# A hand-scheduled attention and FFN kernel: another written order of all steps, and one of four PSUM copies given to ScalarE

## The chip, the cores and the metric

The kernel runs on one core of one Trainium2 chip. The metric is device microseconds of one execution; lower is better. A core has a matrix engine (TensorE, PE in the profile; its weight loads are shown apart as PEld), VectorE (DVE), ScalarE (ACT), GpSimd (POOL) and SyncE (SP, which here only issues DMAs). Each takes its own instructions in the order in which they were written, and waits on semaphores for the others. All of them share 16 DMA engines.

## What is computed

Nystrom attention on q, k, v of shape (8 batches, 8 heads, 576 tokens, 64), followed by a gated FFN without an activation:

```python
q_lm, k_lm = means of 18 rows in a group      # 32 landmarks
A = sm(q, k_lm); Bm = sm(q_lm, k_lm); C = sm(q_lm, k)
Z = start from Bm; six times: Z = 2 * Z - Z @ Bm @ Z
attn = A @ Z @ C @ v
x = attn as (4608, 512)
out = ((x @ w1) * (x @ w2) @ w3) @ w_out      # d_ff 1024
```

## The kernel before, in words

The kernel folds w3 and w_out into one matrix w34, since nothing stands between them, and folds (Z C v) of each batch with w1 and w2 into a matrix G, so that the FFN's two up projections are A times G. All of it is cut into small generators, one for each step; each `yield` ends a part of a step. A string, `ORDER` (lines 32 to 86), lists words such as `U3.1`; the loop at line 661 takes them one by one, starts the word's generator where it stands for the first time and runs it to its next `yield` each time. Nothing else orders the work: on each engine, instructions stand in the order in which the words emit them (`tc.manual_schedule`, line 117), and waits are put in by the framework where buffers or data ask for them.

The words, with the number of their batch or block after the dot:

- `H`, `LO`, `L`, `P`: loads of w3 and w_out in blocks of 128 rows (lines 569, 578, 587, 623; SP's queue, three of them ACT's). w3 blocks go round three places, so block 5 (`L.5`) can only be fetched when block 3 has been transposed (`T0.3`, `T1.3`). `GT` (line 621) is a tiny copy on POOL that reads a loaded block, so that what follows on POOL's queue is not issued before that block is there; the next load into that place also waits for this copy.
- `S`: the split of w_out into two f16 parts (lines 510, 512). `T`: transpose of half a w3 block on PE and its split (lines 525, 529, 531). `F`: product of a block, eight parts of three matmuls, then one copy (lines 539, 542). `K`: one matmul on zeros (line 596); seven more stand ahead of everything.
- `LK`, `LQ`: load of half of k or q of a batch, cast to f16 on the way (line 126, POOL's queue). `TK`, `TQ`: transpose on DVE (line 163). `SK`, `SQ`: landmark sums, on DVE for batch 0 and on POOL for the others (lines 192 to 203). `E`: exchange of landmarks between partitions (lines 210 and 214 for batches 0 and 1; four ACT copies at 221 for the others).
- `B`, `N`, `R`, `I0` to `I5`: Bm, its norms, and the inverse by six iterations (lines 239 to 255, 288, 304, 387 to 406), for the batches of a chain together: (0), (1, 2), (3, 4), (5, 6, 7). A step of `I` is matmuls, then a DVE sum (394), then an ACT copy (400), and the next step's matmuls need both.
- `C`: landmark scores against k (lines 267, 278, 282). `LV`, `FV`: loads of v in four pieces (lines 145, 150, SP's queue). `V`: C v, three parts of PE work (line 344). `Z`: times the inverse (413, 419, 421).
- `A`: scores against the landmarks (323, 330). `M`: their softmax, on DVE (362 to 373).
- `G0` to `G3`: the four blocks of G (line 436: 32 matmuls of a 64x32 shape into a two-bank PSUM tile `big`, then one copy of 128x1024 to f16). `project(st, i)` takes n = i // 2 (the half of d_ff) and w = i % 2 (w1 or w2). G0 and G2 (w = 0) are copied by ACT (line 441), G1 and G3 by DVE (line 443).
- `U0` to `U7`: one eighth of d_ff: four matmuls for w1 into `big` (451), an ACT copy `a_sb` (456), four matmuls for w2, a DVE product (459). U0 to U3 need G0 and G1, U4 to U7 need G2 and G3.
- `W`: 128 rows of the output: eight matmuls (494) in two parts, an ACT copy (500), two DMAs (505). W.35 is cut in two halves (475 to 489).

PSUM holds three `big` tiles and two `one` tiles, so a new `big` waits until an earlier one has been copied out. `qkn` and `vt` have two buffers each.

## Time and profile before

| | |
|---|---|
| runs | 258.41, 258.57 and 256.64 us, median 258.41 us |
| profiled execution | 258.62 us |
| its span, first to last instruction | 256.8 us |
| matmuls on PE | 4448 |
| instructions in all | 10255 |
| read from HBM / written | 38.80 MB / 9.44 MB |
| mean granted clock of PE | 0.993 |

The span is cut into stages by time; "busy" is the union of an engine's instructions in a stage. A row of waits names the instruction that stood idle, what released it, and the idle time. The word "issue" stands where an engine waited for nothing that the profile shows. A row of the timeline gives start, length, engine, line, operation, tiles, and in brackets the idle time before it. The chain of waits follows the end of the execution back, step by step, to what released it.

### The profile page before, as it was taken

What the parts mean: (1) busy time and instruction counts of PE and PEld (TensorE: products, weight loads), DVE (VectorE), ACT (ScalarE), POOL (GpSimd) and SP (SyncE); (2) the same over time, 40 slices, a digit from 0 to 9 for tenths busy, and PEclk for the clock granted to TensorE, in tenths of its full rate; (3) what the DMA queues carried; (4) which work ended last, traced back from release to release, by engine and by line L of the source; (5) the groups of instructions that cost most, each with busy time, mean ns of one, the idle gap of its engine ahead of it and who ended that gap; (6) DMA issues with size and microseconds to landing.
All of it is one profiled execution on the core that took longest, in us unless ns stands there. A gap on an engine that the chain in (4) does not pass through costs nothing.

```text
span 256.8 us, 10255 instructions
## 1 busy us (share of the span) xinstructions
PE 244.3 (95%) x4448; PEld 144.7 (56%) x4448; DVE 182.5 (71%) x348; ACT 140.8 (55%) x317; POOL 117.9 (46%) x199
## 2 busy tenths in 40 slices
PE   7799999997689999999999999999999999999993
PEld 2345545553356646656664766655665646646651
DVE  2689887757658998887998768666958668735410
ACT  4534542457135687766575798457436762654531
POOL 8035799999729996599989930000000000000000
PEclk9799999999999999999999999999999999999999
DMA  6999998999967829799697034444642205313165
GB/s 228 272 309 255 264 246 195 218 222 210 154 94 185 131 35 173 169 204 175 127 189 205 5 89 87 103 123 95 163 96 59 71 3 128 82 42 83 41 146 142
DMA packets 23356, 37.36 MB, mean 145 GB/s; under 512 B 2832, under 2 KB 11536, under 8 KB 23312
## 3 DMA queue, kind: packets, MB, share of 16 engines
q1 hardware_dynamic: 12768, 23.99, 36.8%
q0 software_dynamic: 9792, 11.54, 28.2%
q10 hardware_dynamic: 752, 1.18, 1.5%
q8 instruction: 35, 0.57, 0.9%
q14 instruction: 9, 0.07, 0.1%
HBM read 38.80 MB, written 9.44 MB: 188 GB/s over the span
## 4 chain that ended last, share of the span: by engine, by line
PE 78%; DMA 11%; DVE 4%; issue 2%; SPq 2%; POOL 1%; ACT 0%; POOLq 0%; DVEq 0%
PE big L451 26%; PE one L494 22%; PE one L539 7%; PE big L436 6%; DMA vt<-in_v_dram 5%; PE big L344 5%; DMA qkn<-in_k_dram 5%; PE big L387 4%; PE big L494 1%; PE one L413 1%; PE big L267 1%; PE big L323 1%; SPq L150 1%; DMA out_dram<-o_sb 1%; PE one L304 1%
## 5 line engine op out<-in xcount | busy, mean ns | idle before, releaser
L451 PE MATMUL big<-eat,gt 128*128 128x288 f16 x512 | 75.6, 287 | 3.1 <-issue 3.1
L451 PEld LDWEIGHTS <-gt 128*128 128x128 f16 x512 | 47.7, 98 | 27.4 <-issue 6.9
L456 ACT CAST a_sb<-big 128x576 f16<-128x576 f32 x64 | 40.4, 642 | 41.0 <-PE big L451 30.8
L192 POOL TENSOR_TENSOR tr<-qkT 128x256 f32<-128x256 f16 x56 | 36.1, 673 | 14.6 <-DVE qkT L163 14.1
L494 PE MATMUL one<-w,aby 128*128 128x512 f16 x144 | 36.9, 380 | 0.0
L459 DVE TENSOR_TENSOR abx<-a_sb,big 128x576 f16<-128x576 f16 x32 | 23.6, 748 | 16.7 <-PE big L451 11.8
L539 PE MATMUL one<-abx,w3t 128*128 128x512 f16 x120 | 30.9, 386 | 0.0
L494 PE MATMUL one<-w,abx 128*128 128x512 f16 x120 | 30.2, 379 | 0.0
L459 DVE TENSOR_TENSOR aby<-a_sb,big 128x576 f16<-128x576 f16 x32 | 23.3, 742 | 8.4 <-PE big L451 7.1
L443 DVE TENSOR_SCALAR gt<-big 128x1024 f16<-128x1024 f32 x16 | 19.4, 1218 | 8.0 <-PE big L436 7.9
L163 DVE STREAM_TRANSPOSE qkT<-qkn 128x576 uint32<-128x576 uint32 x32 | 23.9, 756 | 0.9 <-DMA qkn<-in_k_dram 0.9
L500 ACT ACTIVATE o_sb<-one 128x512 f32<-128x512 f32 x33 | 19.6, 600 | 8.3 <-PE one L494 8.3
L494 PEld LDWEIGHTS <-aby 128*128 128x128 f16 x144 | 13.1, 98 | 14.0 <-issue 4.0
L441 ACT ACTIVATE gt<-big 128x1024 f16<-128x1024 f32 x16 | 16.1, 1024 | 8.0 <-PE big L436 7.9
L198 POOL TENSOR_TENSOR tr<-tr 128x256 f32<-128x256 f32 x28 | 20.3, 747 | 0.1
L494 PEld LDWEIGHTS <-abx 128*128 128x128 f16 x136 | 13.0, 98 | 11.8 <-issue 0.4
L436 PE MATMUL big<-wup,zt 64*32 64x512 f16 x512 | 18.8, 379 | 0.0
L539 PEld LDWEIGHTS <-w3t 128*128 128x128 f16 x120 | 11.2, 99 | 12.0 <-issue 0.9
L344 PE MATMUL big<-vt,ent 64*32 64x64 f32 x1152 | 16.2, 223 | 1.6 <-DMA vt<-in_v_dram 1.6
L344 PEld LDWEIGHTS big<-vt,ent 64*32 64x32 f32 x1152 | 13.5, 105 | 6.9 <-issue 5.5
L539 PE MATMUL one<-abx 128*128 128x512 f16 x60 | 16.5, 396 | 0.0
L278 ACT ACTIVATE en<-big 128x288 f32<-128x288 f32 x32 | 12.8, 415 | 4.7 <-PE big L267 4.7
(193 smaller groups left out, 344.8 us busy)
## 6 DMA issues: line engine op xcount, KB each, us to landing
out_dram<-o_sb SPq DMA_DIRECT2D x68, 128.0 KB, 2.4
qkn<-in_k_dram POOLq DMA_DIRECT2D x16, 288.0 KB, 6.5
qkn<-in_q_dram POOLq DMA_DIRECT2D x16, 288.0 KB, 6.6
vt<-in_v_dram SPq DMA_DIRECT2D x16, 288.0 KB, 6.2
vt<-in_v_dram SPq DMA_DIRECT2D x32, 144.0 KB, 4.9
w3f<-in_moe_w_dram SPq DMA_DIRECT2D x5, 512.0 KB, 8.6
wup<-in_moe_w_dram POOLq DMA_DIRECT2D x4, 512.0 KB, 10.8
aby<-in_moe_w_out_dram SPq DMA_DIRECT2D x6, 256.0 KB, 8.2
```

The lines of the kernel that those rows point to most:

```text
L163: nc.vector.transpose(out=st["qkT"][:, t, prs].rearrange("p c r q e -> p (c r q e)").bitcast(U32), in_=st["qkn"][:, t, prs, :].rearrange(" ...
L192: add(out=tr[:, c], in0=x[:, c, 0:4, :], in1=x[:, c, 4:8, :], op=ALU.add)
L198: add(out=tr[:, c, 0:2, :], in0=tr[:, c, 0:2, :], in1=tr[:, c, 2:4, :], op=ALU.add)
L344: nc.tensor.matmul(psV[32 * o:32 * o + 32, qd, 0:64], ent[sl, pr, r, :], vt[sl, pr, 64 * r:64 * r + 64], start=(r == 0), stop=(r == RT - 1 ...
L436: nc.tensor.matmul(psG[o:o + 32, qd, :], zt[rs, i, h, :], wup[rs, h, w, fs], start=(i == 0), stop=(i == 1), tile_position=(64 * qd, o))
L443: nc.vector.tensor_scalar(out=g[:, :, w, fs], in0=psG, scalar1=X64 / ZS, scalar2=None, op0=ALU.mult)
L451: nc.tensor.matmul(p[:, c, 0:HS], st["g"][:, qd, w, 128 * j:128 * j + 128], st["ahat", qd][:, c, :], start=(qd == 0), stop=(qd == 1))
L456: nc.scalar.copy(out=a_sb, in_=p[:, :, 0:HS])
L459: nc.vector.tensor_tensor(out=st["ab"][:, j, st["t0"]:st["t0"] + S].rearrange("p (c s) -> p c s", c=2), in0=a_sb, in1=p[:, :, 0:HS], op=AL ...
L494: nc.tensor.matmul(pso[:, :], ab[:, j, t0:t0 + 128], w34[:, j, :], start=(j == 0), stop=(j == 7))
L500: nc.scalar.activation(out=o_sb, in_=pso, func=AXF.Copy, scale=1.0 / (X64 * X64))
L539: nc.tensor.matmul(psW, w3ts[j, c // 4][:, a, c % 4, :], wsp[:, b, c, :], start=(c == 0 and a + b == 0), stop=(c == 7 and a == 1))
```

## The change

All 53 lines of `ORDER` are written anew. Both orders hold the same words, each the same number of times. One condition in `project` changes: the block with n = 1 and w = 1 (G3) is copied by ACT too. So ACT has three of the four copies of each batch, DVE one.

```diff
 ORDER = """
-H.0 LO.0 KC T0.0 H.3 LO.3 KC LK1.0 H.1 K AT LO.1 T0.0 T0.1 KC S.0 T0.1 H.2 S.0 LO.2 T0.1 T1.0 LQ0.0
-KC F.1 T0.0 S.1 F.0 S.1 LK0.0 S.2 LQ1.0 S.3 T1.0 S.2 T0.0 LO.5 F.1 H.4 K T1.0 T0.0 LO.4 F.0 T0.0
...
-LK0.2 T1.3 F.2 T0.3 E.0 GT.3 TK1.1 F.2 T1.3 P.4 B.0 F.2 FV.0 C.0 B.0 L.5 LQ0.2 B.0 T0.4 F.2 N.0 F.3
...
-T0.7 G0.0 T1.7 B.1 F.6 LK1.4 T1.7 F.6 M1.0 B.1 V.1 G3.0 M1.0 B.1 G0.0 U0.0 F.6 N.1 F.6 G3.0 V.1 G1.0
-U0.0 N.1 U1.0 U1.0 M0.1 F.7 G1.0 R.1 U0.0 TQ1.3 U3.0 R.1 LQ1.4 F.7 U0.0 U3.0 V.1 G2.0 R.1 TQ0.3
...
+H.0 K H.1 H.3 K LO.1 H.4 K LO.4 LO.0 T0.1 LO.2 KC LO.3 T0.0 KC H.2 AT S.0 S.0 K T0.1 GT.0 K T0.0 S.1
+T0.1 KC LO.5 T0.0 T1.1 T0.0 F.0 T1.1 F.1 S.1 L.2 LO.6 F.1 T0.0 T1.0 S.2 LO.7 LK1.0 S.4 T0.0 S.2 T1.1
+LK0.0 GT.2 LQ0.0 S.3 S.3 S.4 T1.0 F.0 F.1 LQ1.0 P.4 T1.0 S.5 LQ1.1 S.6 T0.2 F.0 S.5 F.0 S.7 T0.2 S.6
...
+F.2 LK0.2 F.2 T0.3 E.0 F.2 F.3 F.3 KC TQ0.1 LK1.2 L.5 E.0 LK0.1 B.0 B.0 T1.3 C.0 TQ1.1 F.3 B.0 F.3
+N.0 T0.4 T0.4 N.0 SQ0.1 F.3 C.0 A.0 C.0 R.0 C.0 TK1.1 R.0 F.3 T1.4 R.0 F.3 A.0 I0.0 F.3 A.0 I0.0
+T0.5 T1.4 T0.5 F.4 GT.4 LQ1.2 T1.4 LQ0.2 TK0.1 F.4 I0.0 C.0 M0.0 F.4 FV.0 F.4 T0.5 M0.0 I1.0 I1.0
...
+T1.7 G2.0 G1.0 F.6 G3.0 T0.7 G0.0 E.2 TK1.3 M0.1 C.1 E.2 SK0.3 G1.0 F.7 F.7 G0.0 C.1 B.1 U5.0 M1.1
+LV3.3 G3.0 F.7 V.1 U5.0 U5.0 LK1.4 U1.0 F.7 U5.0 TQ0.3 U1.0 V.1 TK0.4 B.1 U0.0 U1.0 U0.0 F.7 LQ1.4
...
+F.7 I0.1 SK1.3 LQ0.4 U3.0 I0.1 M0.1 TK1.4 F.7 I0.1 I1.1 U4.0 I1.1 I1.1 U4.0 U2.0 U4.0 I2.1 I2.1 I2.1
+U7.0 SQ0.3 I3.1 U2.0 I3.1 U7.0 SQ1.3 I3.1 U6.0 LK0.5 U7.0 U6.0 F.7 LV1.2 U7.0 SK0.4 SK1.4 U6.0 U6.0
...
+SQ0.7 G0.4 U5.3 U2.3 W.9 M0.4 G0.4 C.5 U2.3 SQ1.7 G1.4 W.9 SK0.7 C.5 W.10 M1.4 C.5 U2.3 SK1.7 M0.4
+E.7 U3.3 LV0.5 G1.4 M1.4 U2.3 C.5 E.7 LV0.6 U4.3 B.5 W.9 U3.3 U4.3 U3.3 C.5 B.5 U0.4 U6.3 U3.3 W.10
+U6.3 U6.3 B.5 N.5 U6.3 V.5 V.5 N.5 G3.4 W.13 M0.5 M1.5 LV1.6 U0.4 G3.4 W.11 W.10 U0.4 W.13 M1.5 U3.4
...
 """
...
         yield
-        if w == 0:
+        if w == 0 or n:
             nc.scalar.activation(out=g[:, :, w, fs], in_=psG, func=AXF.Copy, scale=X64 / ZS)
         else:
             nc.vector.tensor_scalar(out=g[:, :, w, fs], in0=psG, scalar1=X64 / ZS,
```

In the new order, PE does the same 4448 matmuls, K among them; the DMAs are the same in number and size, issued in another order on SP's, ACT's and POOL's queues.

## The prediction

> **What bounds the kernel now.** I read the page first, then the busy time by stage, then the waits, and last the timeline at the two stages that the table picked out.

> ```profile
> span 256.8 us, 10255 instructions
> ...
> PE 244.3 (95%) x4448; PEld 144.7 (56%) x4448; DVE 182.5 (71%) x348; ACT 140.8 (55%) x317; POOL 117.9 (46%) x199
> ...
> q8 instruction: 35, 0.57, 0.9%
> ```
> ```profile
> 0.00:12.20 12.20, 8.92 (x30) 4.05 (x31) 5.51 (x17) 5.88 (x11) 5.33 (x19) 0.86 0.87 249
> 60.00:72.00 12.00, 7.24 (x197) 4.06 (x182) 7.14 (x13) 4.10 (x14) 8.78 (x14) 1.00 1.06 177
> 64.30:68.30 4.00, 3.96 (x129) 2.44 (x130) 2.57 (x6) 1.13 (x2) 3.77 (x7) 1.00 1.01 147
> 71.40:250.00 178.60, 178.58 (x3579) 109.70 (x3579) 130.37 (x234) 107.45 (x235) 66.29 (x103) 1.00 0.53 110
> ```
> ```profile
> PE big L451 <- issue: 3.1, 1, 3.1
> ...
> PE big L525 <- DMA w3f<-in_moe_w_dram: 2.0, 1, 2.0
> ...
> PE big L344 <- DMA vt<-in_v_dram: 1.6, 1, 1.6
> ```

> In the stages, the first two numbers are the stage and PE's busy time in it. From 71.4 to 250 us PE is busy 178.58 of 178.60 us: there TensorE is the bound and nothing can be gained by order, only lost. What an order can win lies ahead of that: the start, where PE is busy 8.92 of 12.2 us at a granted clock of 0.86, and the stage from 60 to 72 us, where it is busy 7.24 of 12.

> ```profile
> 62.38 0.32 PE L344 MATMUL big<-vt,ent 64*32 64x64 f32 x10
> 64.32 0.58 PE L344 MATMUL big<-vt,ent 64*32 64x64 f32 x36 [1.62 <-DMA vt<-in_v_dram]
> 67.86 0.42 PE L451 MATMUL big<-eat,gt 128*128 128x288 f16 x2
> 71.42 0.41 PE L451 MATMUL big<-eat,gt 128*128 128x288 f16 x2 [3.14 <-issue]
> ```

> That stage holds two stops of PE: 1.62 us in V.1, until the last piece of v of batch 1 landed, and 3.14 us in the middle of a U, between matmuls that wait for nothing. I take the second for missing instructions: the instruction queue brings 0.57 MB in 35 packets, which is one packet for 127 of the 4448 matmuls, and 129 matmuls ran in the 4.0 us just ahead of the stop, with the DMA engines full (share 1.01). That is an inference; no row names it.

> **The change, part by part.** PE's own work is the same 4448 matmuls. Prices by row, from the chain of waits:

> ```profile
> 65.98 0.65 PE one L539 x3
> ...
> 79.36 0.98 PE big L451 x8
> ...
> 89.81 0.86 PE one L494 x4
> ...
> 94.48 0.56 PE big L436 x16
> ...
> 105.89 0.99 PE big L436 x32
> ...
> 152.83 0.81 PE one L239 x48
> ```

> *Turns between shapes.* Sixteen L436 take 0.56 us, sixteen more 0.43: an entry into the small shapes costs 0.13 us. Counted through the two lists of PE's instructions, turns between full and small shapes go from 120 to 124 (+0.5 us), turns among small shapes from 37 to 32 (up to -0.6 us). I take 0, between -0.6 and +0.5.

> *The wait for v of batch 1.* Ahead of V.1 the new order puts twelve more F matmuls (4 x 0.65 = 2.6 us), 16 each of G2, G1 and G3 (3 x 0.56 = 1.7 us; a whole block is 32, so up to 3 x 0.99 = 3.0) and a U half (0.49): 4.8 to 6.1 us. SP issues the last pieces behind L.7, which waits for GT.5 at the end of about the same POOL work as before. So the wait of 1.62 us is covered three times: -1.6, and 0 if those loads come 6 us later.

> *The instruction stop.* The same count of packets, 128 matmuls each, in the new order: the packet that takes in V.1 holds 38 small ones of G and B, 48 and 18 of V, 12 F and U, and 12 of F, and lasts 6.4 us by these prices against 4.8 in the old order; the shortest between 40 and 100 us lasts 5.2. The old stop began after 4.0 us and ended after 7.1 (71.42 - 64.3). With fewer loads behind it by then I take -3.1. If a packet again takes 7.1 us, 0.7 us of it stays (7.1 - 6.4); if it is no matter of packets, all 3.1 stay.

> *The start.*

> ```profile
> 8.34 1.49 PE L539 MATMUL one<-abx 128*128 128x512 f16 x3
> 9.62 1.49 PE L539 MATMUL one<-abx,w3t 128*128 128x512 f16 x3
> ...
> 13.24 0.81 PE L539 MATMUL one<-abx 128*128 128x512 f16 x3
> ```
> ```profile
> 27.48 0.38 PE L210 MATMUL big<-lm,pick 128*128 128x256 f16 x2 [0.27 <-DVE lm L203]
> ```

> The old start loses 2.0 us for a piece of w3, and six F matmuls at half speed, 2 x (1.49 - 0.81) = 1.4 us. In the new order all pieces of w3 and w_out stand ahead of q and k on the queues (LK1.0 waits for GT.0, LQ0.0 for GT.2), so the weights come sooner and q, k of batch 0 later; 2.4 us more PE work (nine F matmuls and a T) stands ahead of E.0, where PE last waited for VectorE at 27.48. But T0.2 now comes before half of F.0, and waits for a 512 KB block. Best: -3.4; worst: +2.0, the same wait once more. I take -0.6, near the middle.

> [...]

> *SP's queue.* v of batch 0 now stands behind L.5, which waits for T1.3.

> ```profile
> 27.28 9.54 SPq L573 DMA_DIRECT2D w3f<-in_moe_w_dram  x2
> ...
> 43.15 1.10 PE big L344 x72
> ```
> ```profile
> DMA to landing us min/median/max: 4.1/9.3/13.6
> ```

> T1.3 comes about 1.7 us of PE work ahead of E.0, so near 27.5 us, as L.5 did before. Six issues of some 0.65 us end at 31.5, and land 4.1 to 13.6 us later: 35.6 to 45.1, at the median 40.8. V.0 has 1.5 us less PE work ahead of it than before (an F part and two I steps), so stands at 43.15 - 1.5 - 0.6 = 41.0. I take 0, up to +4.1.

> *G3 on ScalarE, and thin places.*

> ```profile
> L443 DVE TENSOR_SCALAR gt<-big 128x1024 f16<-128x1024 f32 x16 | 19.4, 1218 | 8.0 <-PE big L436 7.9
> ...
> L500 ACT ACTIVATE o_sb<-one 128x512 f32<-128x512 f32 x33 | 19.6, 600 | 8.3 <-PE one L494 8.3
> ...
> L441 ACT ACTIVATE gt<-big 128x1024 f16<-128x1024 f32 x16 | 16.1, 1024 | 8.0 <-PE big L436 7.9
> ```
> ```profile
> 149.13 0.41 ACT L278 ACTIVATE en<-big 128x288 f32<-128x288 f32 x1 [0.15 <-PE big L267]
> ...
> 150.04 0.63 ACT L456 CAST a_sb<-big 128x576 f16<-128x576 f32 x1
> ...
> 151.49 1.67 ACT L221 COPY lm<-lm 32x256 f16<-32x256 f16 x4
> ...
> 157.16 0.19 ACT L247 ACTIVATE one<-one 128x32 f32<-128x32 f32 x1
> ...
> 159.30 1.18 ACT L456 CAST a_sb<-big 128x576 f16<-128x576 f32 x2
> ```
> ```profile
> 159.19 0.19 DVE L251 RECIPROCAL rbs<-rbs 128x6 f32<-128x6 f32 x1 [0.59 <-ACT one L247]
> 159.42 0.36 DVE L253 TENSOR_TENSOR bm<-one,rbs 128x192 f32<-128x192 f32 x1
> ```
> ```profile
> 84.02 0.45 PE L387 MATMUL big<-sz__1434,tz__1421 32*32 32x64 f32 x32
> ...
> 85.64 0.45 PE L387 MATMUL big<-sz__1462,tz__1457 32*32 32x64 f32 x32
> ...
> 87.11 0.35 PE L387 MATMUL big<-sz__1511,tz__1497 32*32 32x32 f32 x32
> ```

> VectorE loses 8 x 1.22 = 9.7 us, ScalarE gains 8 x 1.02 = 8.2 us: 149 of 257, still far from full. Neither is at the bound on the whole, so this alone is worth 0; it costs where PE soon needs what lies behind such a copy. Queued behind it are the copies a_sb, and PE for their PSUM. The tightest place I found is N.5, which needs B.5's exponentials. From C.5's matmuls on, ScalarE has U2.3 (0.63), W.9 (0.60), C.5 (2 x 0.91), E.7 (1.67), U3.3 (0.63) and B.5 (157.16 to 159.30, 2.1): 7.5 us, then 0.6 on VectorE: 8.1. PE has G1.4 (0.99), W.10 (1.72), five U halves and one more pair (7 x 0.49 = 3.4) and B.5 (0.81): 6.9. PE waits 1.2 us there. Second, a step of the inverse takes 1.47 to 1.62 us from matmul to matmul; I1.1 to I2.1 to I3.1 in the new order have 0.45 + 0.65 and 0.45 + 0.49 us of PE work on the way from I0.1 and I2.1: 0.4 + 0.5 short. Places with less than 1.3 us of PE work between the release of a `big` and its next use go from 16 to 24; I add 0.2 for them. Short stops: +2.3 in all; at least 0 (ScalarE and VectorE may have run ahead), at most 8.2, each new copy in full.

> **Sum.** -1.6 - 3.1 - 0.6 + 2.3 = -3.0 us. The profiled execution took 258.62 us, 1.8 more than its span, and lies 0.2 over the median of 258.41. So 255.6 us, span 253.8. Within 1% means 255.8 to 261.0, about what a measurement of this kernel can tell from no change.

> **Rivals.**
> 1. The 3.14 us stop stays, there or at another dense place: -1.6 - 0.6 + 2.3 = +0.1, 258.7 us. For it: the packets are inferred. Against it: the thinner packets. [...]
> 2. Slower: ScalarE's in-order queue. G3's copies stand ahead of a_sb copies that PE needs at once. If each of the eight is paid in full, +8.2 in place of +2.3: -5.3 + 8.2 = +2.9, 261.5 us. It decides from 5.3 us of short stops on, 0.66 us a copy. For it: the 1.2 us at N.5. Against it: the old order had stretches where ScalarE was as full, with PE busy 178.58 of 178.60 us.
> 3. v of batch 0 lands last, behind L.5: +4.1 at most, 259.7 us; at 3 us, 258.6. Two fifths of the range of landings lie past 41.0.

> **How the numbers follow.** The forecast has 0.42, rival 1 0.17, rival 3 0.11, rival 2 0.30. Faster by over 1%: 0.42; within 1%: 0.28; slower: 0.30. Low end: all gains (-1.6 - 3.1 - 1.4) and no short stops, 252.5. High end: rival 2's 261.5 and 0.5 for turns, 262.0.

> **What would show it.** Right: no idle PE over 0.5 us between 55 and 75 us, V.1 without a wait for v, PE idle for about 1 us ahead of L288 of the last chain (near 155 us) and twice 0.4 ahead of L387 between 75 and 85. Wrong: an "issue" row of 2 us or more on PE; PE waits for L441 that add up to over 5 us; V.0 waiting for v near 41 us; a PE idle by more than 3 us between 5 and 30 us.

## The result, and the profile after

The changed kernel takes 256.31 us (median of 20 executions, 253.58 to 259.71) where the kernel before takes 257.99 (20 executions, 256.37 to 259.79): a ratio of 0.990, 95% interval 0.987 to 0.993. Unchanged and beside other kernels it was run twice more: 0.989 (0.984 to 0.994) and 0.989 (0.985 to 0.993). So it is faster by about 1%, and the forecast was 255.6. The ratios leave out executions more than 1.5% over the fastest of their kernel, six of these twenty, while the plain medians lie 0.65% apart; the first profiled execution of the changed kernel, 258.57 us, is one of the six and is shown for the stop that it holds.

These are the first lines of its page and its busy time by stage (stage, PE busy, weight loads, VectorE, ScalarE, GpSimd, granted clock, DMA share, GB/s), to be laid beside those of the prediction.

```profile
span 256.8 us, 10254 instructions
...
PE 246.1 (96%) x4448; PEld 146.0 (57%) x4448; DVE 176.3 (69%) x340; ACT 148.1 (58%) x325; POOL 117.0 (46%) x199
```
```profile
0.00:12.20 12.20, 9.76 (x40) 5.24 (x41) 5.47 (x16) 6.33 (x12) 4.15 (x18) 1.00 0.86 287
12.20:55.00 42.80, 41.10 (x552) 22.49 (x551) 36.39 (x78) 17.23 (x42) 30.93 (x51) 1.00 1.10 227
55.00:75.00 20.00, 20.00 (x418) 11.70 (x415) 15.73 (x30) 12.40 (x32) 19.49 (x33) 1.00 0.97 192
```

The stage that held both stops has none now: PE is busy 20.00 of 20.00 us between 55 and 75. The start runs at full clock (1.00, before 0.86). But there is a new stop far behind, as the waits of PE show (line, what ended it, total, times, longest).

```profile
PE big L387 <- issue: 2.0, 1, 2.0
PE big L525 <- DMA w3f<-in_moe_w_dram: 1.2, 1, 1.2
...
PE big L210 <- DVE abx L531: 1.0, 1, 1.0
PE big L344 <- DVE rc L367: 0.7, 1, 0.7
PE big L387 <- ACT sz__1432 L400: 0.2, 1, 0.2
```

This is the timeline of PE at that place, first in this execution, then in the third run of the same kernel, whose profiled execution took 254.37 us.

```profile
127.17 0.35 PE L387 MATMUL big<-sz__2580,tz__2566 32*32 32x32 f32 x30
129.56 0.24 PE L387 MATMUL big<-sz__2580,tz__2566 32*32 32x32 f32 x2 [2.04 <-issue]
129.74 2.09 PE L451 MATMUL big<-eat,gt 128*128 128x288 f16 x8
131.63 1.06 PE L413 MATMUL one<-wbd,xsp 128*128 128x128 f32 x4
```
```profile
126.80 0.35 PE L387 MATMUL big<-sz__2580,tz__2566 32*32 32x32 f32 x32
127.09 1.15 PE L451 MATMUL big<-eat,gt 128*128 128x288 f16 x8
128.08 0.61 PE L413 MATMUL one<-wbd,xsp 128*128 128x128 f32 x4
```

Thirty of one step's 32 matmuls run, PE stands still for 2.04 us with nothing to wait for, and then works at half clock (granted clock 0.50 from 130 to 132 us; eight L451 2.09 against 1.15 us, four L413 1.06 against 0.61). In the other execution none of this happens. The times of the changed kernel lie far apart: in the third run seven executions took 253.6 to 254.7 us and four 256.8 to 257.4 (and one 260.6); of the 38 executions in the three runs 18 took more than 256.5. How much of that is this stop isn't shown: three executions were profiled, and one has it. The twenty of the first run lie without a gap between 253.58 and 259.71, and those of the kernel before are spread by 3.4 us too.

### The profile page after: what moved, and what is told of

Read it like the earlier page. It is cut to its first block, busy times and chain, and to the rows that moved or that the text cites. A ratio compares the mean times of both kernels' runs of the same rounds, so it can differ in the third digit from the quotient of the medians.

```text
span 256.8 us, 10254 instructions
## 1 busy us (share of the span) xinstructions
PE 246.1 (96%) x4448; PEld 146.0 (57%) x4448; DVE 176.3 (69%) x340; ACT 148.1 (58%) x325; POOL 117.0 (46%) x199
## 3 DMA queue, kind: packets, MB, share of 16 engines
q1 hardware_dynamic: 12768, 23.99, 35.6%
q10 hardware_dynamic: 752, 1.18, 1.3%
## 4 chain that ended last, share of the span: by engine, by line
PE 80%; DMA 11%; DVE 3%; issue 3%; POOL 1%; SPq 1%; ACT 1%; ACTq 0%; POOLq 0%
PE big L451 26%; PE one L494 22%; DMA qkn<-in_k_dram 7%; PE one L539 7%; PE big L436 6%; PE big L344 5%; PE big L387 4%; DMA aby<-in_moe_w_out_dram 3%; PE one L413 2%; PE big L494 1%; PE big L267 1%; PE big L323 1%; DMA out_dram<-o_sb 1%; PE big L525 1%; POOL qkn L126 1%
## 5 line engine op out<-in xcount | busy, mean ns | idle before, releaser
L451 PE MATMUL big<-eat,gt 128*128 128x288 f16 x512 | 75.4, 289 | 0.0
L451 PEld LDWEIGHTS <-gt 128*128 128x128 f16 x512 | 48.1, 98 | 22.8 <-issue 2.6
L456 ACT CAST a_sb<-big 128x576 f16<-128x576 f32 x64 | 40.1, 641 | 25.4 <-PE big L451 21.2
L192 POOL TENSOR_TENSOR tr<-qkT 128x256 f32<-128x256 f16 x56 | 35.7, 666 | 17.1 <-DVE qkT L163 16.8
L494 PE MATMUL one<-w,aby 128*128 128x512 f16 x144 | 36.4, 380 | 0.0
L494 PE MATMUL one<-w,abx 128*128 128x512 f16 x120 | 30.2, 380 | 0.0
L539 PE MATMUL one<-abx,w3t 128*128 128x512 f16 x120 | 29.9, 379 | 0.0
L500 ACT ACTIVATE o_sb<-one 128x512 f32<-128x512 f32 x33 | 19.7, 600 | 16.9 <-PE one L494 16.5
L441 ACT ACTIVATE gt<-big 128x1024 f16<-128x1024 f32 x24 | 23.8, 1025 | 8.9 <-PE big L436 8.9
L198 POOL TENSOR_TENSOR tr<-tr 128x256 f32<-128x256 f32 x28 | 20.9, 768 | 0.1
L494 PEld LDWEIGHTS <-aby 128*128 128x128 f16 x144 | 13.1, 98 | 13.1 <-issue 2.5
L494 PEld LDWEIGHTS <-abx 128*128 128x128 f16 x136 | 12.6, 98 | 13.7 <-issue 2.2
L436 PE MATMUL big<-wup,zt 64*32 64x512 f16 x512 | 18.2, 379 | 0.0
L539 PEld LDWEIGHTS <-w3t 128*128 128x128 f16 x120 | 11.4, 98 | 11.1 <-issue 0.4
L344 PE MATMUL big<-vt,ent 64*32 64x64 f32 x1152 | 16.3, 224 | 0.7 <-DVE rc L367 0.7
L344 PEld LDWEIGHTS big<-vt,ent 64*32 64x32 f32 x1152 | 13.6, 105 | 5.4 <-issue 2.8
L539 PE MATMUL one<-abx 128*128 128x512 f16 x60 | 15.6, 380 | 0.0
L369 DVE TENSOR_TENSOR et<-et,rc 128x576 f16<-128x576 f16 x16 | 14.9, 935 | 0.1
L278 ACT ACTIVATE en<-big 128x288 f32<-128x288 f32 x32 | 12.7, 412 | 3.5 <-PE big L267 3.4
```

What stands on the lines that cost most here:

```text
L192: add(out=tr[:, c], in0=x[:, c, 0:4, :], in1=x[:, c, 4:8, :], op=ALU.add)
L198: add(out=tr[:, c, 0:2, :], in0=tr[:, c, 0:2, :], in1=tr[:, c, 2:4, :], op=ALU.add)
L344: nc.tensor.matmul(psV[32 * o:32 * o + 32, qd, 0:64], ent[sl, pr, r, :], vt[sl, pr, 64 * r:64 * r + 64], start=(r == 0), stop=(r == RT - 1 ...
L436: nc.tensor.matmul(psG[o:o + 32, qd, :], zt[rs, i, h, :], wup[rs, h, w, fs], start=(i == 0), stop=(i == 1), tile_position=(64 * qd, o))
L441: nc.scalar.activation(out=g[:, :, w, fs], in_=psG, func=AXF.Copy, scale=X64 / ZS)
L451: nc.tensor.matmul(p[:, c, 0:HS], st["g"][:, qd, w, 128 * j:128 * j + 128], st["ahat", qd][:, c, :], start=(qd == 0), stop=(qd == 1))
```

## The experiments

Each kernel is timed against the kernel before on the same chip, and numbers in the lists of PE count all matmuls from 0. Five runs (old start with new rest, the same with warm-ups moved, new start with old rest, and the two with late loads) carry the words of the order in two lines less, so that L523 there is L525 here, and so on.

**The copy alone.** The old order, and the copies of G3 on ScalarE:

```
-        if w == 0:
+        if w == 0 or n:
```

> The old written order, with the copy of each fourth block of G on ScalarE: the copy change by itself. Theory (the gain is all the order's, the copies are hidden on either engine): the same as before within 0.3%, 257.2 to 258.8 us, and no wait of PE for L441 over 0.5 us. Rival (ScalarE's in-order queue delays the copies behind it): up to 8 x 1.02 = 8.2 us slower, so 259 to 266, with PE waits for ACT rows. Second rival (VectorE was late and the copy change carries part of the gain): 255.5 to 257.

Measured: 265.19 us against 257.24, ratio 1.031 (1.026 to 1.037). The rival has the size right: by itself this line costs 8 us, though PE's longest wait is for VectorE and not for ScalarE. Lists of PE's instructions are the same in both kernels, so each matmul can be laid beside its twin; the rows below are PE's waits, and then ScalarE, VectorE, GpSimd and PE near 107 to 118 us.

```profile
PE big L436 <- DVE gt L443: 2.4, 1, 2.4
...
PE big L451 <- issue: 1.6, 1, 1.6
PE big L387 <- issue: 1.5, 1, 1.5
...
PE one L288 <- DVE bm L253: 0.7, 1, 0.7
PE big L436 <- ACT gt L441: 0.7, 1, 0.7
```
```profile
106.77 1.02 ACT L441 ACTIVATE gt<-big 128x1024 f16<-128x1024 f32 x1 [1.05 <-PE big L436]
107.69 0.19 ACT L247 ACTIVATE one<-one 128x32 f32<-128x32 f32 x1
```
```profile
109.09 0.18 DVE L251 RECIPROCAL rbs<-rbs 128x4 f32<-128x4 f32 x1 [2.40 <-ACT one L247]
...
113.70 3.47 DVE L369 TENSOR_TENSOR et<-et,rc 128x576 f16<-128x576 f16 x1
117.10 1.21 DVE L443 TENSOR_SCALAR gt<-big 128x1024 f16<-128x1024 f32 x1
```
```profile
114.01 2.54 POOL L192 TENSOR_TENSOR tr<-qkT 128x256 f32<-128x256 f16 x4
```
```profile
118.36 0.63 PE L436 MATMUL big<-wup,zt 64*32 64x512 f16 x16 [2.42 <-DVE gt L443]
```

In the kernel before, the same exponentials and the same product stand so:

```profile
105.95 0.18 ACT L247 ACTIVATE one<-one 128x32 f32<-128x32 f32 x1 [0.48 <-PE one L239]
```
```profile
111.61 0.74 DVE L369 TENSOR_TENSOR et<-et,rc 128x576 f16<-128x576 f16 x1
```

There, the exponentials L247 of this chain began at 105.95 us. Now G3's copy stands ahead of them on ScalarE, itself waiting for PE's G matmuls, and they begin at 107.69. VectorE, whose next instruction waits for them, stands idle for 2.40 us, and what stands behind it comes late: the product L369 begins 2.1 us later, and then takes 3.47 us in place of 0.74, so that the copy of G behind it begins at 117.10 and PE waits 2.42 us for it. The product now runs beside GpSimd's sums L192, which began after it in the kernel before, at 114.39. Over all profiles this product takes 0.70 to 0.76 us wherever GpSimd does nothing beside it (99 times), and each of the 61 that took over 1 us ran beside GpSimd's work for at least nine tenths of its time; no run tests this by itself. Without the 2.73 us that it took longer, the copy would have been done at about 115.6 us (an estimate from these rows), before PE came for it at 115.94. So a copy of 1.02 us on ScalarE made VectorE late by some 2 us, and the work that VectorE met there made it a wait of 2.4 us for PE. Steps in which PE falls behind its twin add up to 5.9 us over the list (0.2 to 2.6 us each, eight of them). The rest evens out: a half clock (granted clock 0.91 from 55 to 75 us, 1.00 before) adds 1.6 and a second issue stop 1.5, the first one is 1.5 shorter, and the wait for v of batch 1 isn't there. (These two profiled executions lie 6.4 us apart, the medians on this chip 8.0.)

**The order alone.** The new order, and the copies as before (the line above taken back).

> The new written order with all of those copies on VectorE where they were: the order by itself. Theory (the gain is all the order's): the ratio of the full change, 0.990, within 0.003, so 254.7 to 256.2 us against 258. Rival (the copy change is what makes the new order work): 257 us or more, with PE waits for L443 on VectorE. Rival of the other sign (the copies on ScalarE cost 1 to 2 us of the short stops that were forecast): 253.5 to 254.7.

Measured: 258.64 us, ratio 1.006 (1.002 to 1.009). By itself the order is a little slower too. In the profile VectorE is late at four places:

```profile
PE big L451 <- DVE gt L443: 2.5, 4, 0.9
PE big L387 <- issue: 2.4, 1, 2.4
```
```profile
117.35 1.19 DVE L443 TENSOR_SCALAR gt<-big 128x1024 f16<-128x1024 f32 x1
```
```profile
118.59 1.14 PE L451 MATMUL big<-eat,gt 128*128 128x288 f16 x8 [0.87 <-DVE gt L443]
```

The rival that names the copies is right. The four waits add up to 2.5 us. By the ratios, each to the kernel before on its own chip (1.006 and 0.990), the copies on ScalarE are worth 1.6% with this order, some 4 us; so these waits are more than half of it, and the rest isn't placed. The new order puts U right behind a copy of G which VectorE reaches late and ScalarE in time. So the two parts of the change aren't a sum: +3.1% and +0.6% alone, -1.0% together. Each of the two orders holds for one placing of these copies. (The profiled execution took 263.4 us, more than any but one of its twelve; of it only these rows are used.)

**Old start, new rest, and the reverse.** The words of ORDER for the first 53 us of PE's work from one order, the words that are left from the other; copies as in the kernel that gives the rest.

```
-ORDER = """ H.0 K H.1 H.3 K ... (new)
+ORDER = """ H.0 LO.0 KC T0.0 ... E.2 E.2 F.6 F.6 (old, 53 us) M1.0 M1.0 M0.1 LK0.4 Z.0 ... (the rest, new)
```

> The old order for the first 53 us of PE work, then the steps that are left in the order of the new one, copies as in the new kernel. It keeps the old start (2.0 us wait for w3, 1.7 us lost to a half clock) and has the new order from about 57 us on. Theory A (most of the gain is the two stops in the stage from 60 to 72 us, 1.6 and 3.1 us): 254.5 to 256.5, no stop over 0.5 us between 55 and 75 us. Theory B (most of it is the start): 257 to 258.5.

> The new order for the first 53 us of PE work (up to the last pair of Z.0), then the steps that are left in the old order, copies as before. Theory A (most of the gain is the two stops in the stage from 60 to 72 us, and the start is worth about 1 us): 256.5 to 258.5, with a stop at V.1 for v of batch 1 or an issue stop of 2 to 3 us in the 10 us behind it. Theory B (the start): 255 to 256.5.

Measured: old start with new rest 255.87 us, all but one of its twelve within 255.3 to 256.6, where the kernel before had 257.24; by the ratio, 0.997 (0.994 to 1.000). New start with old rest 260.30, 1.014 (1.009 to 1.019). The first has what theory A names: its time lies in that range, and its profile has no wait of PE over 0.3 us behind the start. But the kernel before is quicker on this chip too, and by the ratio only 0.3% of the 1.0% is left without the new start, as theory B has it. So the two theories stay undecided: the new start is worth nothing by the times, some 2 us by the ratios.

```profile
PE big L523 <- DMA w3f<-in_moe_w_dram: 2.3, 2, 1.9
PE big L594 <- DVE warm L590: 1.2, 1, 1.2
PE big L208 <- DVE lm L201: 0.3, 1, 0.3
PE big L385 <- ACT sz__1432 L398: 0.2, 1, 0.2
```

The second fits neither. It loses 3.1 us at the seam, where PE waits for the exchange of batch 2, which the spliced list brings too late; on what a start is worth it says nothing.

```profile
64.01 0.25 PE L237 MATMUL one<-lm 32*32 32x32 f16 x1 [2.31 <-ACT lm L219]
```

**Old start, new rest, warm-ups moved.** The order of old start and new rest, with four words K moved from behind 12 us to where PE waits for w3:

```
-... H.2 S.0 LO.2 T0.1 T1.0 LQ0.0 ... H.4 K ... GT.0 K S.5 ... L.2 K LK1.1 K T1.1
+... H.2 S.0 LO.2 K K K K T0.1 T1.0 LQ0.0 ...
```

> The old start with the new rest, and four of its warm-up matmuls moved from 12 to 15 us to about 6 us, where PE waits 1.95 us for w3 and then runs at half clock for 3.4 us. Theory (the half clock follows from that idle time): no half clock at 8 to 12 us, F matmuls there at 0.81 us for three instead of 1.4 to 1.5, so 1.4 to 1.7 us less, and 4 x 0.22 to 0.38 us less of warm-up work behind it: 253.0 to 254.5 us where old start and new rest took 255.87. Rival (the clock goes by something else, or PE then waits for w3 anyhow): 255.5 to 256.2.

Measured: 256.41 us against 258.31, 0.992 (0.990 to 0.995), a time above both ranges. The start is as the theory has it: PE's waits for w3 add up to 1.3 us (the longest 0.8; 2.3 and 1.9 without the moved warm-ups), the half clock at 8 to 12 us is gone (granted clock 1.00 in the first 12.2 us, 0.86 without them) and the third group of F matmuls begins 1.3 us sooner, at 10.16 us. But PE then waits 0.8 us for VectorE's `abx` near 19 us and twice for `wup` (1.0 us) between 60 and 64, and by 66 us it is 1.1 us later than in the execution without the moved warm-ups: what PE gained at the start was lost in this execution to what arrives at its own time. Whether the kernel gains isn't decided, since the two ran on different chips: by the ratios (0.992 and 0.997) it is 0.5% quicker, by the times 0.5 us slower.

**The borders between packets of instructions.** Two of the seven first warm-up matmuls are replaced by 64 small ones, which moves all that follows by 62 places in PE's list; no data is added.

```
-    for _ in range(7):
+    for _ in range(5):
         warm_up()
+    for n in range(64):
+        h = 32 * (n % 4)
+        nc.tensor.matmul(psw[h:h + 32, 0, 0:64], warm[h:h + 32, 0:32],
+                         warm[h:h + 32, 0:64], start=True, stop=True, tile_position=(h, h))
```

> The kernel before, with two of its seven first warm-up matmuls replaced by 64 matmuls of 32x32 tiles, 64 columns wide, which moves every later instruction of PE by 62 matmuls (124 instructions) in its list and adds no data. Theory (the 3.14 us issue stop is the wait for the next packet of 128 matmuls with their weight loads, whose border lay at the 855th matmul, 86 past a multiple of 128): no stop at that U matmul; borders now lie at old numbers 792 and 920, and a stop there is 0 to 1.5 us, so 255 to 257 us. Rival (the stop belongs to that place, by load or by a semaphore that the profile does not show): 3 us at the same matmul, 257 to 258.5 us.

> The changed kernel with the same 62 matmuls more at its start. Theory (packets): the issue stop at the 2257th matmul (L387 of an inverse step, 2.0 to 2.4 us) is gone from that place; if one appears it lies 60 to 66 matmuls away from it, or at a like distance from another border. Time 253.5 to 255.5 us if no border falls on a dense place, up to 257 if one does. Rival (the stop belongs to the place): 2 us at the same matmul, 255.5 to 257 us.

Beside them on the same chip the changed kernel itself:

> The changed kernel once more, nothing edited, beside the three kernels that follow. Theory (the order needs the copies on ScalarE, each by itself costs): 0.985 to 0.993 of the time before, so 254.5 to 256.5 us, against 258.6 us for the order alone. Rival (the two chips differ, and the order alone was no slower than the full change there): over 257 us. In the profile: an issue stop of PE of about 2 us at the same matmul as before (the two first L387 of the inverse on tiles sz__2580, tz__2566, the 2257th matmul of PE's list), or none; no PE stop for L443.

And on another chip, with the 64 small matmuls behind the fifth K, where PE is idle anyhow:

> The changed kernel with 64 small matmuls behind its last warm-up matmul, in the place near 7 us where PE waits 1.2 to 1.8 us for w3; all borders between packets of instructions shift by 64 matmuls, and the start isn't lengthened. Theory (the stop belongs to a border): no stop at the matmul that was the 2257th; 254 to 255.5 us where the other borders find no dense place; any issue stop has its place, counted in matmuls, at 80 to 90 past a multiple of 128. Rival (place and not border): as the changed kernel, with its 2 us stop.

Measured: the old order shifted 258.75 us, 1.002 (0.999 to 1.005); the new order shifted 256.48, 0.995 (0.992 to 0.999); the changed kernel beside them 256.42, 0.989; the shift in the idle place 256.46, 0.993 (0.990 to 0.996). In no profile of a shifted kernel is there a stop at the old places; of the new order that alone says little, since two of three profiles of the changed kernel have none either. In the old order shifted the 3.14 us are gone, and other stops of the same kind have come:

```profile
PE big L350 <- issue: 1.1, 1, 1.1
PE one L539 <- DVE abx L512: 1.1, 1, 1.1
PE big L344 <- issue: 0.6, 1, 0.6
PE big L323 <- issue: 0.6, 1, 0.6
```

So the theory is right about the place and wrong about the gain; the two shifted new orders aren't quicker than the changed kernel either. Laid beside its twin, the old list shifted is 2.8 us late by 54 us, for these waits and at the start, gains 5.2 us at the two old stops (1.8 of them at V.1, where v has landed by then) and loses 1.8 again behind them: 0.6 us are left. Borders move, and fall on other dense places. The list below has every stop of PE on "issue" over 0.15 us in all fourteen profiled executions: the number of the first matmul behind it, its remainder by 128, when PE stopped and went on, and when the last packet of the instruction queue ahead of that ended.

```
kernel                 matmul  mod 128  stopped  went on   stop   packet ended  from there
before                    854       86    68.28    71.42   3.14          69.96        1.47
changed                  2256       80   127.52   129.56   2.04         128.16        1.40
copy alone                854       86    67.81    69.42   1.61          68.03        1.39
copy alone               2258       82   136.13   137.64   1.52         136.16        1.48
order alone              2256       80   132.27   134.68   2.41         133.26        1.42
new start, old rest      1746       82   110.94   111.41   0.47         110.17        1.24
warm-ups moved           1491       83    96.98    97.17   0.20          95.84        1.33
warm-ups moved           2257       81   129.36   129.65   0.30         128.34        1.31
old order shifted         473       89    45.18    45.79   0.62          44.20        1.59
old order shifted         601       89    51.42    51.99   0.57          50.61        1.37
old order shifted        1621       85    97.84    98.99   1.15          97.48        1.51
new order shifted        1618       82    99.84   100.00   0.16          98.53        1.47
shift in idle place       472       88    44.40    44.62   0.23          43.01        1.61
shift in idle place      1235       83    83.19    83.64   0.45          82.19        1.45
shift in idle place      3531       75   180.48   181.71   1.23         180.22        1.48
```

All fifteen stand at 75 to 89 past a multiple of 128, in lists that are shifted by 62 or 64 as well as in those that aren't, and all end 1.2 to 1.6 us after a packet of instructions has ended. That fits what the prediction inferred, that PE stands without instructions; no row names it.

**Whether loads make the packet late.** In the changed kernel GpSimd issues a q and a k piece (288 KB each) near 123 us, about when the packet for the border at 2256 is fetched (122.44 to 124.88 us in its second and third runs, 127.21 in the first). A kernel issues them one landmark step later, and VectorE's TQ0.7 with them:

```
-... U7.2 LQ0.7 I5.3 ... C.4 LK1.7 U7.2 ... G2.3 SK1.6 A.4 ... U4.2 TQ0.7 M1.3 ...
+... U7.2 I5.3 ... C.4 U7.2 ... G2.3 SK1.6 LQ0.7 LK1.7 A.4 ... G3.3 TQ0.7 SQ1.6 ...
```

> The changed kernel, nothing edited, as the common yardstick of the two kernels that follow on this chip. 0.985 to 0.993 of the time before. If the packet of instructions that PE reaches near 124 us was asked for ahead of the q and k loads that GpSimd issues there, no issue stop and under 255 us; if behind them, a stop of about 2 us at the 2257th matmul and 256 to 259 us.

> The changed kernel with the last two pieces of q and k of batch 7 that GpSimd issues near 122 us issued one landmark step (3.6 us of GpSimd work) later, and the transposition of one of them on VectorE moved back behind it. Theory (the packet near 124 us waits in the DMA engines behind those 0.58 MB): its fetch comes within 1.5 us of the moment it can be asked for, no stop at the 2257th matmul in any execution, so 254 to 256 us and 0.5 to 1.5 us less than the changed kernel on the same chip, with fewer runs above 257; the price may be up to 1 us at the next packet. Rival (the stop has nothing to do with these loads): the same time within 0.3 us, and the stop still there when the profile catches it.

> The kernel with the late q and k loads once more, for a count of its executions. The changed kernel took more than 256.5 us in 18 of the 38 executions timed so far, and the others lie near 254.5 us; with the late loads it was 2 of 12. Theory (those above are the ones in which a packet of instructions came behind the q and k loads): at most 3 of 12 above 256.5 us, median 254 to 255.3. Rival (chance, the loads have nothing to do with it): 5 or 6 of 12, median 255.5 to 256.5.

Measured on one chip: the changed kernel 254.66 us, 0.989 (0.985 to 0.993); with late loads 254.56, 0.988 (0.985 to 0.991); with late loads again, on another chip, 255.27, 0.989 (0.983 to 0.995). The first row is GpSimd's k issue in the execution that stopped, then that of the third run, which didn't, and that of the late loads.

```profile
123.98 0.72 POOL L126 DMA_DIRECT2D qkn<-in_k_dram  x1
```
```profile
123.69 0.72 POOL L126 DMA_DIRECT2D qkn<-in_k_dram  x1
```
```profile
128.66 0.72 POOL L124 DMA_DIRECT2D qkn<-in_k_dram  x1
```

```
kernel, run            k issued  packet's transfer   PE
changed, first          123.98   127.21 to 128.16    stops 2.04 us
order alone             128.71   132.28 to 133.26    stops 2.41 us
changed, second         122.54   122.44 to 123.69    goes on
changed, third          123.69   123.94 to 124.88    goes on
late loads              128.66   125.30 to 126.38    goes on
late loads again        127.16   123.60 to 125.02    goes on
```

Where PE stops the packet comes 3.2 and 3.6 us after the k issue, where it goes on at most 0.25 us after it. Counted from the moment at which PE passes matmul 2128, one border earlier, the packet begins between 0.3 us ahead and 0.8 us behind where PE goes on, and 3.1 and 3.4 us behind where it stops; in the kernel before it was 4.7 us, from matmul 726 at 64.32. The DMA engines were busy for 0.83, 0.89 and 1.00 of these three stretches. A packet that waits behind loads fits all seven executions, but no row shows when it was asked for, and in the third run the k issue (123.69) also lies ahead of matmul 2128 (123.85), and the packet was in time. So what decides the race stays open.

With the late loads 3 of 18 executions took more than 256.5 us, of the changed kernel 18 of 38; by chance alone so uneven a split has odds of 1 in 40, but the count mixes chips, and on the one that both ran on it was 2 of 12 against 5 of 12, which tells nothing by itself. The medians there are the same within 0.1 us, where 0.5 to 1.5 us less was expected. So it isn't shown that the late loads are faster than the change, only that their packet was in time both times that it was seen.

## Why the prediction was right, and where it wasn't

The forecast of 255.6 us lies 0.7 below the median of 256.31, on the right side and in the range. It was a gain of 3.0 us; the medians are 1.7 us apart, and the ratio stands for 2.7. But two of its terms are off by some 2 us and cancel, so part of the closeness is luck.

- *The wait for v of batch 1, -1.6*: right. None of the profiles of the new order has it, and in the three of the changed kernel PE is busy throughout between 55 and 75 us. The 1.62 us belong to that one execution, though: in the copy-alone run, with the same list of PE, V.1 met no wait.
- *The instruction stop, -3.1*: right in its cause and its place, too large in what it brings. That packet comes in time in the new order; the border at 2256 is the next weak place, worth 2.0 to 2.4 us and in one execution a half clock. The prediction had looked for short packets between 40 and 100 us only and found 5.2 us at least; the 128 matmuls ahead of 2256 last 3.1 us in the third run (123.85 to 126.96). Rival 1 ("there or at another dense place") thus came in one of the three profiled executions. If the executions over 256.5 us are of that kind, which isn't shown, it came in about half, and 0.17 for it was too little. The sign "an issue row of 2 us or more" was called a sign of error, and it came.
- *The start, -0.6 (best -3.4)*: the half clock is gone in all three runs, worth the 2 x (1.49 - 0.81) = 1.4 us that were worked out, and the wait for w3 fell from 2.00 to 1.25 us (1.76 in the second run). Given back: 1.03 us at E.0, against 0.27, where VectorE's `abx` comes late, and in one run 0.67 at V.0. In sum -0.7 to -1.4 by these rows. No idle time over 3 us. The low end of the range counts -1.4 for the start, the half clock alone, where the best case worked out was -3.4. No run shows that term by itself; in the three runs the half clock went together with 0.24 to 0.75 us of the wait for w3, and what the profiles show of it stands in the last section.
- *v of batch 0 behind L.5, 0*: right. V.0 was forecast at 41.0 us and began at 39.7 to 40.5; in two of three profiles it waits for nothing, and in none for v.
- *Short stops, +2.3*: measured 0.24 us, at the one step of the inverse, and 0.13 at another. PE never waits for L441. The step that failed is the N.5 count: 8.1 us of ScalarE and VectorE against 6.9 us of PE work. Both were taken from prices; in the first profile, from C.5's matmuls at 152.44 on, ScalarE and VectorE need 7.3 us and PE has 7.47 us of work, so that it arrives just behind the result:

```profile
159.40 0.36 DVE L253 TENSOR_TENSOR bm<-one,rbs 128x192 f32<-128x192 f32 x1
```
```profile
159.91 0.56 PE L288 MATMUL one<-bm,mask 128*128 128x192 f32 x2
```

- *"This alone is worth 0"*, said of the moved copies: wrong twice. With the old order it costs 8 us, by what stands behind the copy on ScalarE (the exponentials that began at 107.69 us, not 105.95), as rival 2 has it. That this is about the worst price (8 x 1.02 = 8.2) is chance: the steps are 0.2 to 2.6 us, the largest came by way of VectorE, and what stood behind the copy there were exponentials and not copies a_sb. With the new order it brings some 4 us by the ratios. Rival 2 named the right danger and judged it by shares of busy time and thin places. What decides is whether the list was laid out for that placing, and the prediction had no step for this.

The ledger, from the profiled execution before to the third run's (span 256.8 to 252.6, -4.2): v -1.6, issue stop -3.1, w3 -0.75, E.0 +0.8, half clock -1.4, inverse +0.4; -5.7 in all. The 1.5 us that are missing lie in PE's busy time: 244.5 us against 244.3, although it no longer runs at half clock. Turns between shapes were allowed up to 0.5 of it; the rest isn't placed. In the second run PE is busy for 243.3 us, so executions of one kernel differ by as much.

## What to carry to other kernels

An order written out by hand and the choice of the engine for each copy are one decision: test each part alone before you take either for free, since here both parts lose and the whole wins. When PE stops on "issue" in a stretch of many small matmuls, count matmuls to the stop, look for the same remainder elsewhere, and look at which loads were issued ahead of the next packet of instructions; here all fifteen stops stood at 75 to 89 past a multiple of 128, and removing the stop at one border let others show. Executions of one kernel lay up to 6 us apart here, and chips by 1 us, so take several executions, hold each kernel against the one beside it on the same chip, and don't read a gain of 1% from one profile.

## What the runs showed of the hardware

*Packets of instructions.* The instruction queue brings 0.57 MB in 35 packets, in the kernel before and in the changed one alike, one for 127 of the 4448 matmuls. All fifteen stops of the list lie 75 to 89 matmuls past a multiple of 128 and last until 1.24 to 1.61 us after a packet ended; the longest is 3.14 us. Most borders pass unseen: the profile before and the first of the changed kernel have one such stop over 0.15 us each.
